# Attention and two feed-forwards: the sign in the weight conversion, and blocks cut by unit

## The chip, the cores and the metric

The kernel runs on one core of one Trainium2 chip. The metric is the device time of one launch in microseconds (us). Before the change three runs gave 1076.47, 1080.43 and 1082.78 us, so the median is 1080.43 us. The core has five engines with their own in-order instruction streams: TensorE (PE: matrix products; PEld is its weight load), VectorE (DVE), ScalarE (ACT), GpSimd (POOL), and SyncE (SP), which here does nothing but issue DMAs.

## The reference

Inputs arrive as 64-bit floating-point numbers. Block-causal attention (4 batches, 8 heads, 576 positions, head size 64, blocks of 64) is followed by two feed-forwards on 2304 tokens with 512 channels and 2048 hidden channels:

```
scores = q @ k.T / sqrt(64);  masked where block(i) < block(j);  attn = softmax(scores);  x = attn @ v
h = x @ moe_w_in;   g = max(0.01 * h, h);                       x = g @ moe_w_out
h = x @ moe2_w_in;  P = a0 + a1 h + a2 h^2 + a3 h^3;  Q = 1 + |b0| |h| + |b1| h^2
out = (P / (Q + 1e-6)) @ moe2_w_out
```

## The kernel before

**Weights.** A weight stays 64 bits wide in memory, and the kernel reads it as two 32-bit words: `hi` (sign, exponent, upper mantissa) and `lo`. It makes a 32-bit float of them and splits this into a rounded part (`w1i`, `w1o`, or `ch` on its way to the memory tensor `w2h`) and a residual `cl` (on its way to `w1l` or `w2l`). The products run on these parts, three per product: high by high, high by low, low by high.

**Conversion.** `convert` works on 64 blocks of 128 x 512 weights: 32 of the first feed-forward, then 32 of the second. One block passes through these steps:
1. a DMA (L148) loads the block into `cs`, of which there are three;
2. the `hi` words, read as floats, are multiplied by 2^-112, in the first 16 blocks by GpSimd (L166), in the other 48 by ScalarE (L168); this moves the exponent and keeps the sign in the top bit;
3. ScalarE scales the `lo` words as integers (L172);
4. VectorE takes the sign bit out of `hi` and puts it into `lo` (L179, the sign operation);
5. VectorE shifts `hi` left by 3 and joins it with `lo` to the float `cl` (L181);
6. ScalarE rounds it (L184), GpSimd subtracts the rounded part (L185);
7. a DMA issue (L156) writes the residual out; of the second feed-forward both parts are written.

`convert` is a generator with two stops per block: steps 2 to 4 are issued ahead of one stop, 5 to 7 behind it (step 4 belongs to the block before). Between the steps of attention `pace` advances it by a table of due steps (`due`). If a unit of the first feed-forward is prepared before its weights are there, `cv_to` advances it further.

**Blocks before.** A block of the input weights is 128 rows by 512 columns: 128 pieces of 4 KB are read. Four such blocks (all 512 rows) serve four units, so a unit waits for a group of four blocks (table `NEED`). A residual is written in 512 pieces of 512 bytes, four to each partition. A block of the second matrix is 128 full rows.

**Attention and the first feed-forward.** 32 heads run one after the other. Per head: scores (`T`, L291 for the first eight heads, L297 after), maxima on VectorE (`nm`, L303), exponentials on ScalarE (`PB`, L309), division by the sums on GpSimd (L319), transposes (L346), copies of the transposed parts (`pTh` on ScalarE, `pTl` on VectorE, L331 to L339), and the product with v (L374, L378), whose result goes to `xh` and `xl` (L391, L392) or first to `vr` (L394, L395). When a batch's eight heads are done, its first feed-forward (`moe1`, products L455) fills TensorE between the steps of the next batch's heads. It has 32 units per batch, "in" (128 hidden channels) and "out" (128 output channels over 512 hidden ones). For each the residual `wl` is loaded by a DMA on SyncE's queue (L429). The products' results pass through ScalarE (L468, a parametric ReLU with slope 0.01, and L469) and VectorE (`gl`, L470; sums `acc`, L475 and L477).

**The second feed-forward** (`moe2`, products L558 and L612) follows when everything above is done, from about 680 us.

**Order.** SyncE's queue is in program order. A scheduler at build time sets the order of the other engines; each then runs strictly in it, so that an instruction that waits holds up all that stand behind it.

Of the kernel before, what the change touches and what calls it, by code (L numbers as in the profile page):

```python
# [8 lines left out]
F32 = mybir.dt.float32  # L9
F32R = mybir.dt.float32r  # L10
# [3 lines left out]
AF = mybir.ActivationFunctionType  # L14
ALU = mybir.AluOpType
# [9 lines left out]
def attention_moe_moe_kernel(  # L25
# [46 lines left out]
    cp = ph1.enter_context(tc.tile_pool(name="cp", bufs=2))  # L72
# [22 lines left out]
    w1i = w1.tile([P, KD, DFF], F32R, name="w1i")  # L95
    w1o = w1.tile([P, NF, DM], F32R, name="w1o")
# [11 lines left out]

    W1L = dram.tile([2 * NF, P, KD, P], F32, name="w1l")
    W2H = dram.tile([NF, P, 2 * KD, P], F32, name="w2h")
    W2L = dram.tile([NF, P, 2 * KD, P], F32, name="w2l")
    NSF = 8
    E1 = "pvpapv"
    blocks = []
    for wi, wo, which in ((w1_in, w1_out, 1), (w2_in, w2_out, 2)):
        for g in (0, 1, 4, 2, 5, 3, 6, 7) if which == 1 else (0, 4, 1, 5, 2, 6, 3, 7):
            for r in range(4):
                if g < 4:  # L120
                    src = wi[r * P:(r + 1) * P, 2 * g * 512:2 * (g + 1) * 512]
                    fs = slice(4 * g, 4 * g + 4)
                    if which == 1:
                        dst = w1i[:, r, g * 512:(g + 1) * 512], W1L[fs, :, r, :]
                    else:
                        dst = W2H[fs, :, r, :], W2L[fs, :, r, :]
                else:
                    f = 4 * (g - 4) + r
                    src = wo[f * P:(f + 1) * P, :]
                    if which == 1:  # L130
                        dst = w1o[:, f, :], W1L[NF + 4 * (g - 4):NF + 4 * (g - 3), :, r, :]
                    else:
                        dst = tuple(W[f:f + 1, :, KD:2 * KD, :] for W in (W2H, W2L))
                blocks.append((src, dst, which == 1))
    stage = {}
    QME = "ap"
    WHOLE = 8
    NPG = range(0, 16)
    NPC = range(0)
    XLE = "p"  # L140
    EP = "a"
    XWA = 0
# [2 lines left out]
    def load_block(i):  # L145
        if i < len(blocks):
            stage[i] = cp.tile([P, 512, 2], I32, tag="cs", name="cs", bufs=3)
            nc.sync.dma_start(out=stage[i].rearrange("p n w -> p (n w)"), in_=blocks[i][0])  # L148

    split = []  # L150

    def write_block():
        if split:
            for d, t in split.pop():
                out = d.rearrange("u p c -> p u c") if len(d.shape) == 3 else d.rearrange("u p d c -> p (u d) c")
                nc.sync.dma_start(out=out, in_=t.rearrange("p (u c) -> p u c", c=P))  # L156
            ndone[0] += 1

    def convert():
        load_block(0)  # L160
        load_block(1)
        for i in range(len(blocks) + 1):
            if i < len(blocks):
                hi, lo = stage[i][:, :, 1], stage[i][:, :, 0]
                if i in NPG:
                    nc.gpsimd.tensor_scalar(hi.bitcast(F32), hi.bitcast(F32), 2.0 ** -112, 1.0, ALU.mult, ALU.mult)  # L166
                else:
                    nc.scalar.activation(hi.bitcast(F32), hi.bitcast(F32), AF.Copy, scale=2.0 ** -112)  # L168
                if i in NPC:
                    nc.gpsimd.tensor_scalar(lo, lo.bitcast(U32), 0.875 * 2.0 ** -29, 0.4375, ALU.mult, ALU.add)  # L170
                else:
                    nc.scalar.activation(lo, lo.bitcast(U32), AF.Copy, scale=0.875 * 2.0 ** -29, bias=0.4375)  # L172
            if i > 0:
                s = stage.pop(i - 1)
                _, (dh, dl), kept = blocks[i - 1]
                hi, lo = s[:, :, 1], s[:, :, 0]
                f = cp.tile([P, 512], F32, tag="cl", name="cl", bufs=3)
                wh = dh if kept else cp.tile([P, 512], F32R, tag="ch", name="ch", bufs=2)
                nc.vector.scalar_tensor_tensor(lo, hi, -(2 ** 31), lo, ALU.bitwise_and, ALU.bitwise_or)  # L179
                yield  # L180
                nc.vector.scalar_tensor_tensor(  # L181
                    f.bitcast(I32), hi, 3, lo, ALU.logical_shift_left, ALU.bitwise_or
                )
                nc.scalar.copy(wh, f)  # L184
                nc.gpsimd.tensor_tensor(f.bitcast(F32R), f, wh.bitcast(F32), ALU.subtract)  # L185
                load_block(i + 1)
                write_block()
                split.append(((dh, wh.bitcast(F32)), (dl, f))[kept:])
                yield
        write_block()  # L190
# [60 lines left out]
    def a1(n):  # L251
# [5 lines left out]
        if n < NSF + 2:  # L257
            split_tiles(n)
        e = n % 2
        qs, ks = qk[e][0:D, :], qk[e][D:P, :]  # L260
        cp1(E1[0], QT[e][0:D, :], qs, SCALE)
        nc.vector.scalar_tensor_tensor(
            QT[e][D:P, :], qs, SCALE, QT[e][0:D, :].bitcast(F32), ALU.mult, ALU.subtract
        )
        cp1(E1[2], QM[e][0:D, :], QT[e][0:D, :].bitcast(F32))
        cp1(E1[3], KH[e][D:P, :], ks)
        cp1(E1[4], KH[e][0:D, :], ks)
        (nc.vector if E1[5] == "v" else nc.gpsimd).tensor_tensor(
            KL[e][0:D, :], ks, KH[e][D:P, :].bitcast(F32), ALU.subtract
# [133 lines left out]
    units = []  # L403
    for b in range(B):
        fs = list(range(NF))
        cuts = [5, 9, 13, 16] if b < B - 1 else [5, 10, 14, 16]
        done = 0
        for g, c in enumerate(cuts):
            units += [(b, "in", f, 0) for f in fs[done:c]]
            done = c  # L410
            units += [(b, "out", g, d) for d in range(KD)]
    NEED = {
        ("in" if g < 4 else "out", g % 4): 4 * (n + 1) for n, g in enumerate((0, 1, 4, 2, 5, 3, 6, 7))
    }
    wt = {}
    prepped = [0]

    def prep_w1(u):
        while prepped[0] <= min(u, len(units) - 1):
            w = prepped[0]  # L420
            ub, kind, i, d = units[w]
            if ub == 0:
                cv_to(NEED["in", i // 4] if kind == "in" else NEED["out", i])
            if kind == "in":
                wh, src = w1i[:, :, i * P:(i + 1) * P], W1L[i]
            else:
                wh, src = w1o[:, 4 * i:4 * i + 4, d * P:(d + 1) * P], W1L[NF + 4 * i + d]
            wl = mp.tile([P, 4, P], F32R, tag="wl", name="wl", bufs=3)
            nc.sync.dma_start(out=wl.bitcast(F32), in_=src)  # L429
            wt[w] = (wh, wl)  # L430
            prepped[0] += 1
# [208 lines left out]
    with tc.manual_schedule(engines={mybir.EngineType.SP}):  # L640
# [50 lines left out]
        for n, (b, h) in enumerate(heads):  # L691
            odd, p = h % 2, n // 2
# [49 lines left out]
        for i in range(16):  # L742
# [3 lines left out]
            if L0 <= i < L0 + NA + 2:  # L746
                f = i - L0
# [49 lines left out]
```

## Time and profile before

| | |
|---|---|
| median of 3 runs | 1080.43 us |
| profiled execution | 1077.4 us, its span 1075.6 us |
| TensorE busy | 1015.4 us (94%) |
| VectorE busy | 770.2 us (72%) |
| ScalarE busy | 661.4 us (61%) |
| GpSimd busy | 314.2 us (29%) |
| mean granted TensorE clock | 0.986 |

The conversions begin at 19.4 us and end near 527 us. Attention with the first feed-forward between its steps ends near 570 us; the rest of the last batch's first feed-forward runs until about 680 us, and the second feed-forward after it. The granted clock is the share of full speed that TensorE was given: 1.0 is 2.4 GHz, 0.5 is 1.2 GHz. "Idle before" counts the time in which an engine had no instruction running, and the engine and line behind the arrow ended it.

### The profile page before, as it was taken

The page shows a single profiled execution, that of the slowest core. Times are in us where ns is not written, and L with a number is a line of the kernel's source. Part 1 is how long each engine was busy: PE and PEld are TensorE (multiplying, and loading weights), DVE is VectorE, ACT ScalarE, POOL GpSimd, SP SyncE. Part 2 cuts the span into 40 slices and gives each one's busy share as a digit, 9 for nine tenths or more (in the row PEclk, how much of TensorE's full clock was granted, in tenths as well). Part 3 has the DMA queues.
Part 4 walks back from the last instruction along what each step waited for, and adds up shares of the span by engine and source line. Part 5 has one row for each costly group of instructions (what it writes and reads, how often), then busy time and mean ns, then how long its engine had stood idle before and what let it go on. Part 6 is the DMA issues. An engine that isn't in the chain of part 4 may idle for free.

```text
span 1075.6 us, 16845 instructions
## 1 busy us (share of the span) xinstructions
PE 1015.4 (94%) x6120; PEld 911.1 (85%) x6120; DVE 770.2 (72%) x1261; ACT 661.4 (61%) x1319; POOL 314.2 (29%) x368
## 2 busy tenths in 40 slices
PE   6878888898999999999999999899999999999998
PEld 4557888898989999999999999788888888888887
DVE  3778778886767775877632222698988888888876
ACT  5766656855756665666632111777776676676675
POOL 5687545555444555545320001100000000000000
PEclk9999899999999999999999999999999999999999
DMA  7458566856766567665445845812000110110010
GB/s 190 135 150 252 155 192 189 261 169 203 218 190 175 185 201 237 200 196 168 145 132 197 329 127 171 340 56 79 4 36 9 70 40 1 40 40 1 1 40 20
DMA packets 99954, 149.01 MB, mean 139 GB/s; under 512 B 8224, under 2 KB 52256, under 8 KB 99872
## 3 DMA queue, kind: packets, MB, share of 16 engines
q1 hardware_dynamic: 99872, 147.95, 43.7%
q8 instruction: 48, 0.79, 0.3%
q14 instruction: 34, 0.28, 0.1%
HBM read 108.01 MB, written 39.32 MB: 137 GB/s over the span
## 4 chain that ended last, share of the span: by engine, by line
PE 53%; issue 11%; DMA 8%; DVE 6%; ACT 3%; POOL 2%; SPq 1%; POOLq 0%; ACTq 0%; DVEq 0%
PE o L612 18%; PE h L558 18%; PE M L455 12%; DMA cs<-in_moe_w_in_dram 4%; DMA cs<-in_moe_w_out_dram 3%; PE T L297 2%; PE T L346 2%; PE T L378 1%; POOL acc L482 1%; DVE cl L181 1%; ACT cs L168 1%; ACT cs L172 1%; DVE cs L179 1%; DVE pTl L339 1%; DVE nm L303 1%
## 5 line engine op out<-in xcount | busy, mean ns | idle before, releaser
L319 POOL TENSOR_SCALAR PB<-PB,sm 128x448 f32<-128x448 f32 (+4 forms) x160 | 104.7, 674 | 58.0 <-DVE sm L316 49.5
L309 ACT ACTIVATE PB<-T,nm 128x448 f32<-128x448 f32 (+4 forms) x160 | 83.1, 524 | 55.8 <-DVE nm L303 52.0
L455 PE MATMUL M<-gh,wl 128*128 128x288 f32 x512 | 114.0, 299 | 1.1 <-DMA wl<-w1l 1.1
L455 PE MATMUL M<-gh,w1o 128*128 128x288 f32 x512 | 113.8, 300 | 1.3 <-DVE pTl L339 0.6
L455 PE MATMUL M<-gl,w1o 128*128 128x288 f32 x512 | 111.6, 298 | 1.0 <-DVE gl L470 1.0
L570 ACT ACTIVATE ea<-h,coef 128x512 f32<-128x512 f32 (+1 forms) x80 | 51.7, 647 | 92.7 <-PE h L558 88.9
L470 DVE TENSOR_TENSOR gl<-M,gh 128x576 fp32r<-128x576 f32 x64 | 47.8, 749 | 65.7 <-ACT M L469 65.6
L558 PE MATMUL h<-x2h,w2h 128*128 128x512 f32 (+1 forms) x240 | 89.6, 373 | 4.1 <-DVE eu L581 3.2
L455 PE MATMUL M<-xh,w1i 128*128 128x288 f32 x512 | 84.6, 299 | 8.5 <-DVE pTl L339 3.8
L179 DVE SCALAR_TENSOR_TENSOR cs<-cs 128x512 int32<-128x512 int32 x64 | 60.1, 938 | 44.7 <-ACT cs L172 33.2
L558 PE MATMUL h<-x2h,w2l 128*128 128x512 f32 (+1 forms) x240 | 89.4, 373 | 0.0
L558 PE MATMUL h<-x2l,w2h 128*128 128x512 f32 (+1 forms) x240 | 89.3, 372 | 0.0
L455 PE MATMUL M<-xl,w1i 128*128 128x288 f32 x512 | 86.0, 301 | 2.2 <-DVE xl L392 1.3
L468 ACT ACTIVATE gh<-M 128x576 fp32r<-128x576 f32 x64 | 41.7, 652 | 75.3 <-PE M L455 75.0
L303 DVE TENSOR_REDUCE nm<-T 128x1 f32<-128x448 f32 (+4 forms) x160 | 71.5, 479 | 21.7 <-PE T L291 13.5
L573 DVE SCALAR_TENSOR_TENSOR ea<-eh,coef,ea 128x512 f32<-128x512 f32 (+1 forms) x80 | 55.9, 699 | 41.4 <-ACT eh L571 40.8
L455 PEld LDWEIGHTS M<-gh,wl 128*128 128x128 f32 x512 | 83.6, 190 | 1.6 <-DMA wl<-w1l 1.6
L455 PEld LDWEIGHTS M<-gh,w1o 128*128 128x128 f32 x512 | 83.0, 190 | 2.2 <-ACT w1i L184 0.8
L612 PE MATMUL o<-w2h,g2l 128*128 128x512 f32 x216 | 84.9, 393 | 0.0
L612 PE MATMUL o<-w2h,g2h 128*128 128x512 f32 x216 | 84.8, 393 | 0.0
L612 PE MATMUL o<-w2l,g2h 128*128 128x512 f32 x216 | 84.6, 392 | 0.0
L455 PEld LDWEIGHTS M<-gl,w1o 128*128 128x128 f32 x512 | 83.1, 190 | 1.3 <-DVE gl L470 1.3
(113 smaller groups left out, 2614.9 us busy)
## 6 DMA issues: line engine op xcount, KB each, us to landing
wl<-w1l SPq DMA_DIRECT2D x128, 256.0 KB, 3.0
cs<-in_moe_w_in_dram SPq DMA_DIRECT2D x32, 512.0 KB, 5.3
cs<-in_moe_w_out_dram SPq DMA_DIRECT2D x32, 512.0 KB, 4.6
w1l<-cl SPq DMA_DIRECT2D x32, 256.0 KB, 5.0
w2h<-ch SPq DMA_DIRECT2D x32, 256.0 KB, 4.9
w2l<-cl SPq DMA_DIRECT2D x32, 256.0 KB, 5.1
w2h<-w2h SPq DMA_DIRECT2D x12, 512.0 KB, 7.4
w2l<-w2l SPq DMA_DIRECT2D x12, 512.0 KB, 8.1
```

The costliest lines, as they stand in the source:

```text
L179: nc.vector.scalar_tensor_tensor(lo, hi, -(2 ** 31), lo, ALU.bitwise_and, ALU.bitwise_or)
L297: nc.tensor.matmul(T[:, po:po + w], lhsT=lhs[e][:, FIRST[i]:FIRST[i] + P], rhs=rhs[e][:, c:c + w], start=(lhs is QT), stop=(lhs is QM),)
L303: nc.vector.tensor_reduce(nm[:, i:i + 1], sc, axis=AX.X, op=ALU.max, negate=True)
L309: nc.scalar.activation(PB[e][i][:, 0:ln], sc, AF.Exp, scale=SCALE if n == 0 else 1.0, bias=nm[:, i:i + 1], accum_out=sm[:, i:i + 1])
L319: nc.gpsimd.tensor_scalar(PB[e][i][:, 0:ln], PB[e][i][:, 0:ln], sm[:, i:i + 1], 1.0, ALU.mult, ALU.mult)
L455: nc.tensor.matmul(T[:, e * 512:e * 512 + NH2], lhsT=w[:, kk, :], rhs=a[:, e * NH2:(e + 1) * NH2], start=(n == 0), stop=(n == 11),)
L468: nc.scalar.activation(gh2, res, AF.Prelu, alpha=0.01)
L470: nc.vector.tensor_tensor(gl2, res, gh2.bitcast(F32), ALU.subtract)
L558: nc.tensor.matmul(h[:, 0:n], lhsT=a, rhs=x, start=(kk == 0 and i == 0), stop=(kk == KD - 1 and i == 2))
L570: nc.scalar.activation(a, h, AF.Abs, scale=coef[:, 4:5])
L573: nc.vector.scalar_tensor_tensor(a, h2, coef[:, 5:6], a, ALU.mult, ALU.add)
L612: nc.tensor.matmul(ob[t], lhsT=a, rhs=w, start=(f == 0 and i == 0), stop=(f == NF - 1 and i == 2))
```

## The change

Three things change in `convert` and what feeds it.

- ScalarE scales the `hi` words of all 64 blocks by a parametric ReLU. The scale is 2^-112 and the slope for negative values -(2^32). A positive word comes out as before. A negative one comes out positive, with its exponent 32 higher; shifted left by 3, that bit of the exponent is the sign bit. The sign operation of VectorE (L179) goes, and the joining operation (L181 before) reads `hi` and `lo` as scaled.
- In the first 16 blocks GpSimd now scales the `lo` words instead of the `hi` words.
- A block is what one unit uses: 512 rows by 128 columns of either matrix of the first feed-forward, listed in the order of the units (32 blocks). Of the second feed-forward a block is 512 rows by 128 columns of the input matrix, or 128 full rows of the output matrix, in turns. Loads of the first three kinds (48 blocks) are in 512 pieces of 1 KB, and every residual and every part of the second feed-forward's weights is written in 128 pieces of 2 KB. A unit of the first batch waits for its own block (`cv_to(w + 1)`).

```
     E1 = "pvpapv"
+    CUTS = [5, 9, 13, 16]
     blocks = []
-    for wi, wo, which in ((w1_in, w1_out, 1), (w2_in, w2_out, 2)):
-        for g in (0, 1, 4, 2, 5, 3, 6, 7) if which == 1 else (0, 4, 1, 5, 2, 6, 3, 7):
-            for r in range(4):
-                if g < 4:
-                    src = wi[r * P:(r + 1) * P, 2 * g * 512:2 * (g + 1) * 512]
...
-                blocks.append((src, dst, which == 1))
+    for g, c in enumerate(CUTS):
+        for f in range(CUTS[g - 1] if g else 0, c):
+            src = w1_in[:, 2 * f * P:2 * (f + 1) * P].rearrange("(r p) w -> p r w", p=P)
+            blocks.append((src, (w1i[:, :, f * P:(f + 1) * P], W1L[f]), True))
+        for d in range(KD):
+            src = w1_out[512 * g:512 * (g + 1), 2 * d * P:2 * (d + 1) * P].rearrange("(r p) w -> p r w", p=P)
+            blocks.append((src, (w1o[:, 4 * g:4 * g + 4, d * P:(d + 1) * P], W1L[NF + 4 * g + d]), True))
+    for f in range(NF):
+        src = w2_in[:, 2 * f * P:2 * (f + 1) * P].rearrange("(r p) w -> p r w", p=P)
+        blocks.append((src, (W2H[f, :, 0:KD, :], W2L[f, :, 0:KD, :]), False))
+        src = w2_out[f * P:(f + 1) * P, :].rearrange("p (r w) -> p r w", r=KD)
+        blocks.append((src, (W2H[f, :, KD:2 * KD, :], W2L[f, :, KD:2 * KD, :]), False))
...
-    NPG = range(0, 16)
-    NPC = range(0)
...
-            nc.sync.dma_start(out=stage[i].rearrange("p n w -> p (n w)"), in_=blocks[i][0])
+            nc.sync.dma_start(out=stage[i].rearrange("p (r n) w -> p r (n w)", r=KD), in_=blocks[i][0])
...
-                out = d.rearrange("u p c -> p u c") if len(d.shape) == 3 else d.rearrange("u p d c -> p (u d) c")
-                nc.sync.dma_start(out=out, in_=t.rearrange("p (u c) -> p u c", c=P))
+                nc.sync.dma_start(out=d, in_=t)
...
-                if i in NPG:
-                    nc.gpsimd.tensor_scalar(hi.bitcast(F32), hi.bitcast(F32), 2.0 ** -112, 1.0, ALU.mult, ALU.mult)
-                else:
-                    nc.scalar.activation(hi.bitcast(F32), hi.bitcast(F32), AF.Copy, scale=2.0 ** -112)
-                if i in NPC:
+                nc.scalar.activation(
+                    hi.bitcast(F32), hi.bitcast(F32), AF.Prelu, scale=2.0 ** -112, alpha=-(2.0 ** 32)
+                )
+                if i < 16:
                     nc.gpsimd.tensor_scalar(lo, lo.bitcast(U32), 0.875 * 2.0 ** -29, 0.4375, ALU.mult, ALU.add)
                 else:
                     nc.scalar.activation(lo, lo.bitcast(U32), AF.Copy, scale=0.875 * 2.0 ** -29, bias=0.4375)
...
-                f = cp.tile([P, 512], F32, tag="cl", name="cl", bufs=3)
-                wh = dh if kept else cp.tile([P, 512], F32R, tag="ch", name="ch", bufs=2)
-                nc.vector.scalar_tensor_tensor(lo, hi, -(2 ** 31), lo, ALU.bitwise_and, ALU.bitwise_or)
+                f = cp.tile([P, KD, P], F32, tag="cl", name="cl", bufs=3)
+                wh = dh if kept else cp.tile([P, KD, P], F32R, tag="ch", name="ch", bufs=2)
+                hi, lo = (x.rearrange("p (r c) -> p r c", c=P) for x in (hi, lo))
                 yield
                 nc.vector.scalar_tensor_tensor(
                     f.bitcast(I32), hi, 3, lo, ALU.logical_shift_left, ALU.bitwise_or
                 )
...
-        cuts = [5, 9, 13, 16] if b < B - 1 else [5, 10, 14, 16]
+        cuts = CUTS if b < B - 1 else [5, 10, 14, 16]
...
-    NEED = {
-        ("in" if g < 4 else "out", g % 4): 4 * (n + 1) for n, g in enumerate((0, 1, 4, 2, 5, 3, 6, 7))
-    }
...
-                cv_to(NEED["in", i // 4] if kind == "in" else NEED["out", i])
+                cv_to(w + 1)
```

Line numbers of the changed kernel are smaller by 4 to 9: the joining operation is L175 there, the maxima L297, `pTl` L333, `gl` L461, `vr` L389, the reciprocal L310.

VectorE before, from 112 to 119 us of the trace (the fourth row is the sixteenth sign operation, whose block is the last that GpSimd scales; `cs` holds the words, `cl` the joined float, `gl` a residual of the first feed-forward, `vr` an attention output):

```order
L316 RECIPROCAL sm<-sm 128x5
L470 TENSOR_TENSOR gl<-M,gh 128x576
L181 SCALAR_TENSOR_TENSOR cl<-cs 128x512
L179 SCALAR_TENSOR_TENSOR cs<-cs 128x512
L181 SCALAR_TENSOR_TENSOR cl<-cs 128x512
L395 TENSOR_TENSOR vr_87<-T,vr_87 64x576
L470 TENSOR_TENSOR gl<-M,gh 128x576
L276 TENSOR_TENSOR VHL_96<-vr_86,VHL_96 128x5x64
```

VectorE in the changed kernel at the same `vr`:

```order
L175 SCALAR_TENSOR_TENSOR cl<-cs 128x512
L310 RECIPROCAL sm<-sm 128x5
L461 TENSOR_TENSOR gl<-M,gh 128x576
L175 SCALAR_TENSOR_TENSOR cl<-cs 128x512
L389 TENSOR_TENSOR vr_87<-T,vr_87 64x576
L461 TENSOR_TENSOR gl<-M,gh 128x576
L270 TENSOR_TENSOR VHL_96<-vr_86,VHL_96 128x5x64
```

Of the four conversion instructions ahead of this `vr` before, both sign operations are gone (the other one stood three rows above this piece); the joining operation of the same block still stands directly ahead of `vr`.

VectorE before, around the transposed parts of a head in the second batch (the 43rd sign operation, at 316.04 us of the trace):

```order
L336 TENSOR_TENSOR pTh<-T,pTh 64x128
L339 TENSOR_TENSOR pTl<-T,pTh 128x768
L339 TENSOR_TENSOR pTl<-T,pTh 128x448
L179 SCALAR_TENSOR_TENSOR cs<-cs 128x512
L339 TENSOR_TENSOR pTl<-T,pTh 128x320
L181 SCALAR_TENSOR_TENSOR cl<-cs 128x512
L470 TENSOR_TENSOR gl<-M,gh 128x576
L303 TENSOR_REDUCE nm<-T 128x1 x2
```

VectorE in the changed kernel at the parts of the same head:

```order
L330 TENSOR_TENSOR pTh<-T,pTh 64x128
L333 TENSOR_TENSOR pTl<-T,pTh 128x768
L175 SCALAR_TENSOR_TENSOR cl<-cs 128x512
L333 TENSOR_TENSOR pTl<-T,pTh 128x448
L461 TENSOR_TENSOR gl<-M,gh 128x576
L333 TENSOR_TENSOR pTl<-T,pTh 128x320
L297 TENSOR_REDUCE nm<-T 128x1 x2
```

The sign operation between the second and third `pTl` is gone. The joining operation of the block before stands between the first and second, and that of this block five rows behind this piece.

## Rows read from the trace of the kernel before

**Rows 1.** The page: busy us (share of span) xinstructions.
```profile
PE 1015.4 (94%) x6120; PEld 911.1 (85%) x6120; DVE 770.2 (72%) x1261; ACT 661.4 (61%) x1319; POOL 314.2 (29%) x368
```

**Rows 2.** Stages: length, busy us by engine, PEclk, DMA share, GB/s.
```profile
10.00:200.00 190.00, 159.01 (x959) 136.01 (x958) 144.59 (x241) 126.26 (x288) 121.04 (x140) 0.95 0.62 188
200.00:570.00 370.00, 353.16 (x2591) 343.60 (x2591) 256.43 (x423) 231.27 (x494) 182.18 (x200) 0.99 0.62 188
```

**Rows 3.** TensorE's waits, 10 to 570 us: total us, times, longest.
```profile
PE T L297 <- DVE vr L395: 9.7, 6, 4.0
...
PE T L346 <- POOL PB L319: 7.1, 10, 4.1
...
PE M L455 <- DMA wl<-w1l: 1.1, 1, 1.1
...
PE T L378 <- DVE acc L329: 0.2, 1, 0.2
```

**Rows 4.** Groups, 0 to 560 us: busy us, mean ns | idle before.
```profile
L179 DVE SCALAR_TENSOR_TENSOR cs<-cs 128x512 int32<-128x512 int32 x64 | 60.1, 938 | 44.7 <-ACT cs L172 33.2 <-POOL cs L166 11.2
...
L181 DVE SCALAR_TENSOR_TENSOR cl<-cs 128x512 int32<-128x512 int32 x64 | 57.7, 903 | 1.1
...
L168 ACT ACTIVATE cs<-cs 128x512 f32<-128x512 f32 x48 | 32.6, 680 | 42.5 <-DMA cs<-in_moe_w_in_dram 24.3 <-DMA cs<-in_moe_w_out_dram 18.1
...
L468 ACT ACTIVATE gh<-M 128x576 fp32r<-128x576 f32 x48 | 31.3, 652 | 5.8 <-PE M L455 5.5
...
L166 POOL TENSOR_SCALAR cs<-cs 128x512 f32<-128x512 f32 x16 | 13.7, 858 | 5.3 <-DMA cs<-in_moe_w_in_dram 5.2
...
L185 POOL TENSOR_TENSOR cl<-cl,w1o 128x512 fp32r<-128x512 f32 x16 | 22.3, 1402 | 20.4 <-ACT w1o L184 18.5 <-issue 1.8
```

**Rows 5.** VectorE's timeline at 115.91: start, us, what [idle].
```profile
115.91 1.74 DVE L179 SCALAR_TENSOR_TENSOR cs<-cs 128x512 int32<-128x512 int32 x1 [2.47 <-POOL cs L166]
```

**Rows 6.** TensorE's timeline, first instruction behind four gaps.
```profile
30.94 0.64 PE L291 MATMUL T<-fk,fq 128*128 128x448 f32 x1 [1.79 <-DVE xl L392]
...
119.09 1.11 PE L297 MATMUL T<-split_fk,split_fq 128*128 128x448 f32 x2 [4.02 <-DVE vr L395]
...
317.28 0.90 PE L455 MATMUL M<-xh,w1i 128*128 128x288 f32 x5 [1.97 <-DVE pTl L339]
...
503.50 0.52 PE L297 MATMUL T<-split_fk,split_fq 128*128 128x192 f32 x3 [1.86 <-DVE pTl L339]
```

**Rows 7.** VectorE's timeline, 316 to 317 us.
```profile
316.04 0.69 DVE L179 SCALAR_TENSOR_TENSOR cs<-cs 128x512 int32<-128x512 int32 x1 [3.27 <-ACT cs L172]
316.65 0.48 DVE L339 TENSOR_TENSOR pTl<-T,pTh 128x320 fp32r<-128x320 f32 x1
```

**Rows 8.** ScalarE's waits, 0 to 570 us: total us, times, longest.
```profile
ACT cs L168 <- DMA cs<-in_moe_w_in_dram: 24.3, 13, 4.0
ACT cs L168 <- DMA cs<-in_moe_w_out_dram: 18.1, 11, 3.5
```

**Rows 9.** Stages, first and last of five at half clock.
```profile
76.77:83.60 6.83, 5.42 (x13) 3.30 (x13) 6.75 (x13) 3.16 (x11) 3.56 (x6) 0.50 0.22 31
...
264.50:267.92 3.42, 3.42 (x17) 3.42 (x16) 0.84 (x2) 1.44 (x3) 2.21 (x2) 0.50 0.82 269
```

**Rows 10.** DMA issues: count, KB each, median us to landing.
```profile
wl<-w1l SPq DMA_DIRECT2D x128, 256.0 KB, 3.0
...
cs<-in_moe_w_in_dram SPq DMA_DIRECT2D x32, 512.0 KB, 5.3
...
w1l<-cl SPq DMA_DIRECT2D x32, 256.0 KB, 5.0
...
x2hd<-xo SPq DMA_DIRECT2D x16, 288.0 KB, 2.5
...
vr<-in_v_dram SPq DMA_DIRECT2D x16, 256.0 KB, 3.0
...
x2l<-x2ld SPq DMA_DIRECT2D x4, 1024.0 KB, 7.7
```

More of the change, by code (lines that the diff above doesn't have):

```diff
@@ L115, in attention_moe_moe_kernel @@
     E1 = "pvpapv"
+    CUTS = [5, 9, 13, 16]
     blocks = []
-    for wi, wo, which in ((w1_in, w1_out, 1), (w2_in, w2_out, 2)):
-        for g in (0, 1, 4, 2, 5, 3, 6, 7) if which == 1 else (0, 4, 1, 5, 2, 6, 3, 7):
-            for r in range(4):
-                if g < 4:
-                    src = wi[r * P:(r + 1) * P, 2 * g * 512:2 * (g + 1) * 512]
-                    fs = slice(4 * g, 4 * g + 4)
-                    if which == 1:
-                        dst = w1i[:, r, g * 512:(g + 1) * 512], W1L[fs, :, r, :]
-                    else:
[L126 to L133, printed above, removed]
-                blocks.append((src, dst, which == 1))
+    for g, c in enumerate(CUTS):
[10 more added lines that the diff above has]
+        blocks.append((src, (W2H[f, :, KD:2 * KD, :], W2L[f, :, KD:2 * KD, :]), False))
     stage = {}
@@ L164, in convert @@
                 hi, lo = stage[i][:, :, 1], stage[i][:, :, 0]
-                if i in NPG:
-                    nc.gpsimd.tensor_scalar(hi.bitcast(F32), hi.bitcast(F32), 2.0 ** -112, 1.0, ALU.mult, ALU.mult)
-                else:
-                    nc.scalar.activation(hi.bitcast(F32), hi.bitcast(F32), AF.Copy, scale=2.0 ** -112)
-                if i in NPC:
+                nc.scalar.activation(
+                    hi.bitcast(F32), hi.bitcast(F32), AF.Prelu, scale=2.0 ** -112, alpha=-(2.0 ** 32)
+                )
+                if i < 16:
                     nc.gpsimd.tensor_scalar(lo, lo.bitcast(U32), 0.875 * 2.0 ** -29, 0.4375, ALU.mult, ALU.add)
```

## The prediction, made before the change was run

> **What bounds the kernel now.** I read the page first, then a table by stage, then who ends TensorE's waits, then the rows around those waits.
>
> TensorE is busy for 1015.4 of 1075.6 us [rows 1], so a change can only give back its idle time and the time it runs at the lower of its two clock levels. The table by stage shows where both lie: busy 159.0 of 190 us from 10 to 200 us and 353.2 of 370 from there to 570 us, that is 31.0 + 16.8 = 47.8 us idle, and granted clocks of 0.95 and 0.99 there [rows 2]. All 64 weight conversions run in this stretch; behind it nothing is converted and this change has nothing to move.
>
> Who ends these waits: fourteen rows name VectorE, from 9.7 us down to 0.2 us, together 29.3 us; the other engines end less (GpSimd 7.1 us at most in a row), and a DMA of the second operand `wl` 1.1 us [rows 3]. VectorE is not full. It is late because it works strictly in order and a conversion stands in its way: the sign operation (L179) runs 64 times for 60.1 us and VectorE sits idle for 44.7 us ahead of it, until ScalarE or GpSimd has scaled the words. The operation behind it (L181, 57.7 us) has 1.1 us of idle time [rows 4].
>
> Two places show how that reaches TensorE. At 115.91 L179 has kept VectorE idle for 2.47 us, until GpSimd's L166; it runs 1.74 us, L181 and `vr` (L395) are queued behind it [rows 5], and TensorE has idled 4.02 us for that `vr` [rows 6]. At 316.04 L179 starts after 3.27 us of idle time, until ScalarE's L172, and the 0.48 us of `pTl` behind it [rows 7] end 1.97 us of TensorE [rows 6].
>
> I went back from every TensorE gap of over 0.5 us between 10 and 570 us by the same steps. There are 26, 40.3 us together. In 21 of them, from the one that ends at 30.94 to the one that ends at 503.50 [rows 6], L179 lies on the chain; they hold 32.7 us. The other five (a coefficient load at the start, two queues of GpSimd, a ScalarE wait, a `wl` load) the change does not touch.
>
> **The change part by part.** The profiled execution took 1077.4 us (span 1075.6); the runs have a median of 1080.43, so it lies 3.0 us under that and inside their spread. The sum is made against 1077.4.
>
> *The sign operation goes.* 64 instructions, 60.1 us of VectorE, and the place at which VectorE waits. In each of the 21 gaps I take the smaller of the gap and L179's own runs on its chain: 25.7 us. If the wait ahead of it goes too, all 32.7 us go. The changed order gives the wait back at the later of the two places (nothing of the conversion stands between the second and third `pTl` any more), but not at the earlier one: there the joining operation still stands ahead of `vr` and still waits for GpSimd.
>
> What is late next differs. In nine gaps (16.0 us whole, 15.5 by the runs) the chain goes back through VectorE and GpSimd; with the one at 119.09 cut to its 1.74 us, since GpSimd's word stays in its place, I take 13.7 us. In twelve (16.7 whole, 10.3 by the runs) it goes back through ScalarE's in-order wait for a weight load ahead of L168, 24.3 + 18.1 = 42.4 us in 24 waits [rows 8], which the change keeps; there `pTh`, `PB` or `gh` on ScalarE is late next, and I take half of the runs, 5.2 us. Sum 18.9.
>
> *The clock.* Five stretches at half clock (1.2 GHz), 23.9 us long together, start around the ends of the five gaps at 76.34, 119.09, 141.53, 199.21 and 263.85, all with a conversion on their chain; TensorE is busy 21.1 us in them, first and last shown [rows 9]. At 2.4 GHz that work takes half, so at most 10.6 us come back. Shorter gaps, not none, are forecast, so I take half: 5.3.
>
> *Float scaling goes from GpSimd (16 blocks) and ScalarE's Copy (48) to a parametric ReLU on ScalarE; the integer scaling of 16 blocks goes to GpSimd.* ScalarE trades 16 instructions against 16. A parametric ReLU is in the trace: 652 ns for 128x576 against 680 ns of L168 for 128x512 [rows 4], so 64 of them cost between 1.8 us less and nothing more: 0 taken. GpSimd's integer form isn't shown. Nearest is L166, 858 ns, dearest L185 with its two inputs, 1402; so between 0 and 16 x 0.54 = 8.7 us more; a gain is left out, since L166 has the same shape and the same pair of operations. I take 0, by L166; the cover is GpSimd's slack (121.0 busy of 190 us, [rows 2]), and without it up to 8.7 us come on the path, between 20 and 115 us.
>
> *The fused operation waits later.* It now waits for ScalarE and GpSimd itself; queued behind it are `vr`, `xl`, `pTl` and the maxima `nm`, which TensorE and the exponentials wait for. That is the same queue that L179 held up, half a conversion step later, by when ScalarE is mostly past it: 0, and the upper end is the gap between 25.7 and 32.7 already left out.
>
> *Blocks of one unit.* Units need one block instead of four at once; TensorE has hardly waited for it (1.1 us for `wl`, at the end of the stage, [rows 3]): 0. The loads come in pieces of 1 KB instead of 4 KB (48 of 64), the residuals go out in pieces of 2 KB instead of 512 bytes. For loads the rows bound it: 256 KB take 3.0 us in pieces of 512 bytes (`vr`) and 3.0 in pieces of 2 KB (`wl`): nothing, and no row shows more pieces as faster; at the dear end the slowest load with as many pieces, `x2l`, takes 7.7 us against 5.3 of the weights: +2.4 [rows 10]. Twelve gaps of 16.7 us hang on those 42.4 us, 0.39 us of TensorE for each. I take +0.4 us, near the first pair, in the 24 waits there are: 24 x 0.4 x 0.39 = 3.8 us lost. Writes are off TensorE's path: 0, though `w1l` at 5.0 us against 2.5 for `x2hd` [rows 10] leaves something to gain.
>
> The Trainium skill ("DMA: Bandwidth & Descriptors", Specifications) puts the least size for full rate at 512 bytes; by it neither the loads nor the writes would change, and the sum would be 3.8 us better. The pair `vr`, `wl` agrees for loads. The pair `w1l`, `x2hd` does not for writes.
>
> Sum: 18.9 + 5.3 - 3.8 = 20.4 us. 1077.4 - 20.4 = 1057.0, and at the level of the median 1080.4 - 20.4 = 1060.0; the profile lies under its median by less than the runs scatter, so I name 1059.
>
> **The rivals.**
> - *The waits only move* (no change). The fused operation takes over L179's 44.7 us of waiting, and what VectorE saves is idle time. For it: the words it waits for are made no sooner. Against it: it stands later in VectorE's order. Only the gaps without a wait ahead of L179 (four, ending at 80.03, 94.16, 172.25 and 182.91) would go, 3.9 us, and no clock: 1076.5.
> - *The loads in 1 KB pieces* (slower). Each load lands later and ScalarE, in order, waits at the head of every block, with the exponentials and `pTh` behind it. At the dear end, 24 x 2.4 x 0.39 = 22.5 us lost; the twelve gaps then give nothing and the clock half of its share: 22.5 - 13.7 - 2.6 = 6.2 us slower, 1087. It decides from loads 16.3/(24 x 0.39) = 1.7 us later on; under that the kernel is faster. Against it: the pair of rows with equal landing times.
> - *GpSimd's integer form is dear.* 8.7 us on the path, at the half of the span where it is fullest: 1068.
> - *All of it comes back*: 32.7 + 10.6 = 43.3 us, 1037. Against it: the ScalarE waits for loads stay.
> - *The ReLU does not come cheap* (a table load each time): excluded nearly, since the same function already runs among the exponentials with 5.5 of its 5.8 us of idle time owed to TensorE [rows 4].
>
> **How the numbers follow.** The forecast 0.55, all of it 0.12, GpSimd dear 0.11, waits only move 0.13, loads slow 0.09. What runs can tell from no change is about 0.5%, 5.4 us. Faster: 0.55 + 0.12 + 0.11 = 0.78. Same: 0.13. Slower: 0.09. The range goes from 1041, most of the way to the best case, to 1079, which takes in the unchanged case but not the slow one. The forecast's own range is 1049 to 1068.
>
> **What would show it.** Right: VectorE's instructions fall by 64 and its busy time by 55 to 65 us; idle time ahead of the fused operation under 25 us; TensorE's idle time from 10 to 570 us near 28 us; fewer stretches at half clock before 300 us. GpSimd's integer scaling under 1 us, the ReLU near 0.68, weight loads landing within 0.5 us of 5.3. Wrong: idle time of 40 us before the fused operation (the waits moved), ScalarE waiting over 60 us for weight loads (the pieces), or GpSimd's scaling at over 1.3 us.

## The result, and the profile after

The change makes the kernel faster by about 12 us: four runs have a median of 1066.05 us (1062.72 to 1071.16), before it was 1080.57; the ratio of the two kernels is put at 0.9885 with a 95% interval of 0.985 to 0.9919, that is 8.8 to 16.2 us (the medians alone lie 14.5 us apart). The forecast was 1059 with a range of 1041 to 1079: the direction and the range held, the gain by the ratio was 60% of the 20.4 us worked out.

The changed kernel's page, busy time by engine, beside [rows 1]:

```profile
PE 1012.0 (95%) x6120; PEld 908.7 (85%) x6120; DVE 714.5 (67%) x1197; ACT 658.7 (62%) x1319; POOL 300.8 (28%) x368
```

VectorE has 64 instructions and 55.7 us less, as counted on. The span fell from 1075.6 to 1064.6 us: TensorE's busy time by 3.4 us, its idle time by 7.6.

The stages, with the columns of [rows 2], and the first and the last of the three stretches at half clock that are left of the five (both kernels have one more near 16 us, ahead of the conversions):

```profile
10.00:200.00 190.00, 170.72 (x1059) 147.82 (x1057) 126.59 (x228) 137.13 (x312) 123.38 (x147) 0.96 0.66 206
200.00:565.00 365.00, 345.24 (x2548) 336.63 (x2547) 221.11 (x375) 220.72 (x475) 166.43 (x193) 1.00 0.59 183
78.10:84.90 6.80, 6.25 (x24) 4.88 (x23) 4.28 (x11) 4.61 (x12) 4.76 (x7) 0.50 1.01 351
...
252.20:255.60 3.40, 3.40 (x17) 3.40 (x16) 0.04 (x1) 1.25 (x3) 1.05 (x1) 0.50 0.94 349
```

Up to 200 us TensorE idles 190 - 170.7 = 19.3 us, 11.7 less than before. Behind that it idles 365 - 345.2 = 19.8 us, 3.0 more. So the gain lies in the first 200 us, and a part of it is given back later.

The conversion's own rows, with the columns of [rows 4]:

```profile
L175 DVE SCALAR_TENSOR_TENSOR cl<-cs 128x512 int32<-128x512 int32 x64 | 51.1, 799 | 72.2 <-DMA w2l<-cl 26.8 <-ACT cs L166 25.5 <-POOL cs L164 14.7
...
L160 ACT ACTIVATE cs<-cs 128x512 f32<-128x512 f32 x64 | 43.4, 678 | 58.3 <-DMA cs<-in_moe_w_out_dram 31.2 <-DMA cs<-in_moe_w_in_dram 26.9
...
L164 POOL TENSOR_SCALAR cs<-cs 128x512 int32<-128x512 uint32 x16 | 12.6, 787 | 3.6 <-DMA cs<-in_moe_w_in_dram 2.0 <-DMA cs<-in_moe_w_out_dram 0.5
```

The parametric ReLU costs 678 ns, what Copy cost, and GpSimd's integer form 787 ns, under the 858 of its float form. But VectorE's idle time ahead of the joining operation is 72.2 us, where the sign operation had 44.7: the waits did not go, they moved to the operation that is left, and 26.8 us of waiting for a free residual buffer came to them. ScalarE's waits for weight loads rose from 42.4 to 58.1 us. TensorE's idle time from 10 us to the end of the conversions is 39 us; the prediction had named 28, before it was 47.8.

What ScalarE's wait for a load does now, at 339 us: ScalarE, VectorE and TensorE in order of time (start, us, what, idle before):

```profile
336.42 0.67 ACT L160 ACTIVATE cs<-cs 128x512 f32<-128x512 f32 x1 [3.31 <-DMA cs<-in_moe_w_out_dram]
336.99 0.89 ACT L325 CAST pTh<-T 128x896 fp32r<-128x896 f32 x1
```
```profile
337.91 0.28 DVE L330 TENSOR_TENSOR pTh<-T,pTh 64x128 fp32r<-64x128 f32 x1 [4.35 <-ACT pTh L325]
338.21 0.96 DVE L333 TENSOR_TENSOR pTl<-T,pTh 128x768 fp32r<-128x768 f32 x1
```
```profile
339.31 0.64 PE L291 MATMUL T<-split_fk,split_fq 128*128 128x192 f32 x4 [1.59 <-DVE pTl L333]
```

ScalarE stands 3.31 us at the head of a block, `pTh` is queued behind it, `pTl` needs `pTh`, and TensorE loses 1.59 us. VectorE had nothing to do for 4.35 us. Before, at 316 us, such a wait reached TensorE through the sign operation [rows 7].

The DMA issues, beside [rows 10]:

```profile
cs<-in_moe_w_in_dram SPq DMA_DIRECT2D x32, 512.0 KB, 4.9
cs<-in_moe_w_out_dram SPq DMA_DIRECT2D x32, 512.0 KB, 5.7
w1l<-cl SPq DMA_DIRECT2D x32, 256.0 KB, 4.9
```

### The profile page after: what moved, and what is told of

Same layout as the page of the kernel before. It is cut to its first block, busy times and chain, and to the rows that moved or that the text cites. A ratio compares the mean times of both kernels' runs of the same rounds, so it can differ in the third digit from the quotient of the medians.

```text
span 1064.6 us, 16750 instructions
## 1 busy us (share of the span) xinstructions
PE 1012.0 (95%) x6120; PEld 908.7 (85%) x6120; DVE 714.5 (67%) x1197; ACT 658.7 (62%) x1319; POOL 300.8 (28%) x368
## 4 chain that ended last, share of the span: by engine, by line
PE 47%; issue 15%; DMA 13%; ACT 8%; DVE 7%; POOL 6%; SPq 4%; POOLq 0%; DVEq 0%; ACTq 0%
PE o L603 19%; PE h L549 18%; PE M L446 7%; DMA cs<-in_moe_w_out_dram 5%; DMA w2l<-cl 3%; DMA cs<-in_moe_w_in_dram 2%; POOL PB L313 2%; ACT PB L303 2%; PE T L340 1%; DMA x2hd<-xo 1%; ACT cs L160 1%; SPq L235 1%; PE T L372 1%; ACT cs L166 1%; POOL cl L179 1%
## 5 line engine op out<-in xcount | busy, mean ns | idle before, releaser
L313 POOL TENSOR_SCALAR PB<-PB,sm 128x448 f32<-128x448 f32 (+4 forms) x160 | 92.2, 596 | 60.4 <-DVE sm L310 49.7
L175 DVE SCALAR_TENSOR_TENSOR cl<-cs 128x512 int32<-128x512 int32 x64 | 51.1, 799 | 72.2 <-DMA w2l<-cl 26.8
L461 DVE TENSOR_TENSOR gl<-M,gh 128x576 fp32r<-128x576 f32 x64 | 48.1, 754 | 72.3 <-ACT M L460 70.9
L564 DVE SCALAR_TENSOR_TENSOR ea<-eh,coef,ea 128x512 f32<-128x512 f32 (+1 forms) x80 | 55.7, 696 | 43.2 <-ACT eh L562 42.6
L446 PE MATMUL M<-xh,wl 128*128 128x288 f32 x512 | 82.4, 298 | 2.3 <-DMA wl<-w1l 2.3
L340 PE MATMUL T<-ident,PB 128*128 128x128 f32 x480 | 70.5, 285 | 14.5 <-POOL PB L313 7.1
```

Source lines behind the costliest of these rows:

```text
L175: nc.vector.scalar_tensor_tensor(f.bitcast(I32), hi, 3, lo, ALU.logical_shift_left, ALU.bitwise_or)
L313: nc.gpsimd.tensor_scalar(PB[e][i][:, 0:ln], PB[e][i][:, 0:ln], sm[:, i:i + 1], 1.0, ALU.mult, ALU.mult)
L340: nc.tensor.transpose(T[:, c:c + P], PB[e][i][:, kt * P:(kt + 1) * P], ident)
L446: nc.tensor.matmul(T[:, e * 512:e * 512 + NH2], lhsT=w[:, kk, :], rhs=a[:, e * NH2:(e + 1) * NH2], start=(n == 0), stop=(n == 11),)
L461: nc.vector.tensor_tensor(gl2, res, gh2.bitcast(F32), ALU.subtract)
L564: nc.vector.scalar_tensor_tensor(a, h2, coef[:, 5:6], a, ALU.mult, ALU.add)
```

## The experiments

Every kernel ran in rounds beside the kernel before; ratios are to that kernel, 1080 us.

| run | what it is | ratio (95%) |
|---|---|---|
| | the change | 0.9885 (0.985 to 0.9919) |
| e1 | sign alone moved | 0.9827 (0.9797 to 0.9857) |
| e2 | blocks alone | 1.0035 (1.0017 to 1.0053) |
| e3 | sign operation kept, issued late | 0.9978 (0.9962 to 0.9994) |
| e4 | the change, loads one block earlier | 0.9784 (0.9755 to 0.9812) |
| e5 | e1 with an extra operation of two inputs | 0.9949 (0.993 to 0.9967) |
| e6 | e1 with an extra maximum of `hi` | 0.9884 (0.9851 to 0.9918) |
| e7 | e1, loads one block earlier | 0.9812 (0.9786 to 0.9838) |
| e8 | e7, residuals written earlier | 0.9849 (0.9829 to 0.9869) |
| e9 | before, loads one block earlier | 0.9978 (0.9961 to 0.9995) |
| e10 | e2, loads one block earlier | 0.9979 (0.9955 to 1.0003) |
| e11 | the change, GpSimd scales nothing | 0.9821 (0.9794 to 0.9848) |
| e12 | e1 with an extra maximum of `cl` | 0.9895 (0.9872 to 0.9918) |

**The two halves, e1 and e2.** Theory 1: the sign operation is the gain. Theory 2: the blocks are. e1 is the kernel before with

```
-                if i in NPG:
...
-                    nc.scalar.activation(hi.bitcast(F32), hi.bitcast(F32), AF.Copy, scale=2.0 ** -112)
-                if i in NPC:
+                nc.scalar.activation(
+                    hi.bitcast(F32), hi.bitcast(F32), AF.Prelu, scale=2.0 ** -112, alpha=-(2.0 ** 32)
+                )
+                if i < 16:
...
-                nc.vector.scalar_tensor_tensor(lo, hi, -(2 ** 31), lo, ALU.bitwise_and, ALU.bitwise_or)
```

> Blocks, loads and waits by groups of four stay as before; only the sign moves into the parametric ReLU (and GpSimd scales the integer words of the first 16 blocks). Theory 1, the freed sign operation is the whole gain: 1064 to 1070 us, ratio to before 0.985 to 0.991, VectorE's busy time 55 us lower. Theory 2, the blocks of one unit make the gain: 1077 to 1082 us, ratio 0.997 to 1.003.

e2 is the changed kernel with the scaling and the sign operation of before put back.

> The sign operation and the scaling stay as before; only the blocks are cut by unit (loads in 1 KB pieces, writes in 2 KB pieces, a unit waits for its own block). Theory 1: 1078 to 1084 us, ratio 0.997 to 1.004, with ScalarE's waits for weight loads near 55 us as in the changed kernel if the pieces cost something. Theory 2: 1064 to 1070 us, ratio 0.985 to 0.991.

Measured: 1063.52 and 1084.44 us. Theory 1 holds: the sign is worth 18.7 us (15.4 to 21.9), and the blocks cost 3.8 (1.8 to 5.7). The product of the two ratios is 0.9861, and the change's 0.9885 has it in its interval. Both times lie just outside what theory 1 had named (1064 to 1070 and 1078 to 1084 us): the sign gains more than the whole change, and the blocks cost. The stages of e1, then of e2, then the second stage of before cut at the same time:

```profile
10.00:200.00 190.00, 168.03 (x1031) 145.48 (x1029) 124.78 (x224) 135.14 (x306) 123.73 (x148) 0.96 0.67 203
200.00:562.00 362.00, 346.67 (x2575) 338.36 (x2575) 221.71 (x378) 224.69 (x480) 165.89 (x192) 1.00 0.61 188
```
```profile
10.00:200.00 190.00, 159.18 (x958) 135.87 (x957) 143.17 (x239) 122.72 (x283) 117.02 (x139) 0.95 0.60 185
200.00:562.00 362.00, 341.35 (x2480) 332.45 (x2481) 260.36 (x421) 229.67 (x493) 174.66 (x198) 0.98 0.58 184
```
```profile
200.00:562.00 362.00, 345.71 (x2535) 336.15 (x2534) 255.64 (x422) 228.88 (x490) 179.32 (x198) 0.99 0.62 187
```

The blocks cost nothing up to 200 us (30.8 us idle, 31.0 before); behind it TensorE idles 20.7 us with them and 16.3 before, and the granted clock is 0.98. In e1 it idles 9.0 us less than before up to 200 us and 1.0 us less behind. ScalarE's groups with the waits for weight loads, e1 first, then e2:

```profile
L165 ACT ACTIVATE cs<-cs 128x512 f32<-128x512 f32 x64 | 43.5, 680 | 59.1 <-DMA cs<-in_moe_w_in_dram 29.6 <-DMA cs<-in_moe_w_out_dram 29.3
```
```profile
L163 ACT ACTIVATE cs<-cs 128x512 f32<-128x512 f32 x48 | 32.6, 678 | 38.9 <-DMA cs<-in_moe_w_out_dram 21.1 <-DMA cs<-in_moe_w_in_dram 17.5
```

So these waits rose with the sign's move and not with the pieces: 58.9 us in e1, whose loads are in 4 KB pieces, and 38.6 in e2, with 48 of 64 loads in 1 KB pieces, against 42.4 before. The expectation of near 55 us in e2 failed, and the blocks' 3.8 us do not come by longer waits of ScalarE for loads. e2 changes the pieces of the loads, the pieces of the writes and what a unit waits for at once; which of them costs was not run by itself.

**Wait or running time: e3, e5, e6, e12.** The prediction held that the sign operation hurt by standing at the head of VectorE's queue. Theory A: its wait is the price. Theory B: its 60 us of running are. e3 moves the operation behind the stop:

```
-                nc.vector.scalar_tensor_tensor(lo, hi, -(2 ** 31), lo, ALU.bitwise_and, ALU.bitwise_or)
                 yield
+                nc.vector.scalar_tensor_tensor(lo, hi, -(2 ** 31), lo, ALU.bitwise_and, ALU.bitwise_or)
```

> The kernel before with the sign operation kept (60 us of VectorE) and only issued behind the stop, right ahead of the joining operation. If the place of the wait held TensorE up: idle time ahead of the sign operation falls from 44.7 us, and the time comes down to 1064 to 1072 us. If the 60 us of running did: 1075 to 1082 us.

Measured: 1077.83 us, but the edit did not do what it was for. The wait ahead of the sign operation stayed, 41.2 us against 44.7 (the group of e3, with the columns of [rows 4]):

```profile
L180 DVE SCALAR_TENSOR_TENSOR cs<-cs 128x512 int32<-128x512 int32 x64 | 58.7, 917 | 41.2 <-ACT cs L172 31.6 <-POOL cs L166 9.0
```

So it tells nothing of the wait. e5 goes the other way: it leaves the sign to the ReLU and adds an operation that waits for nothing, and e6 and e12 one with a single input (each run has one of the three added lines):

```
                 nc.vector.scalar_tensor_tensor(
                     f.bitcast(I32), hi, 3, lo, ALU.logical_shift_left, ALU.bitwise_or
                 )
+                nc.vector.scalar_tensor_tensor(lo, hi, 0, lo, ALU.bitwise_and, ALU.bitwise_or)    # e5
+                nc.vector.tensor_reduce(junk, hi.bitcast(F32), axis=AX.X, op=ALU.max)             # e6
+                nc.vector.tensor_reduce(junk, f, axis=AX.X, op=ALU.max)                           # e12
```

> The kernel with the sign alone moved (1063.5 us), plus one VectorE operation per block right behind the joining one: lo = (hi and 0) or lo, the same shape and two inputs as the old sign operation, with nothing left to wait for. If the 60 us of running were the price of the sign operation: back to 1074 to 1082 us. If its wait at the head of the queue was: 1062 to 1068 us.

> As the run with the extra operation, but the extra one is a maximum over the hi words: one input, about the same VectorE time. If VectorE's own queue is what the running costs: 1074 to 1082 us as there. If the price is that an operation with two inputs holds GpSimd up: GpSimd's divisions keep their 600 ns (670 ns in the run with two inputs) and the time stays at 1062 to 1068 us.

> The sign alone moved (1063.5 us) plus a maximum over the joined words directly behind the joining operation: one input, nothing to wait for, 64 runs of 0.6 to 0.7 us. If VectorE's time itself is the price: near the 1073 us of the extra operation with two inputs, at least 1070. If what two inputs do to GpSimd is: 1062 to 1067 us, GpSimd's divisions near 613 ns.

Measured: e5 1073.41, e6 1067.39, e12 1068.65 us. First e1's groups of the joining operation and of GpSimd's divisions, then those of e5, e6 and e12 with the extra operation:

```profile
L317 POOL TENSOR_SCALAR PB<-PB,sm 128x448 f32<-128x448 f32 (+4 forms) x160 | 95.0, 613 | 52.8 <-DVE sm L314 43.9 <-ACT gh L466 8.4 <-PE T L289 0.2
...
L179 DVE SCALAR_TENSOR_TENSOR cl<-cs 128x512 int32<-128x512 int32 x64 | 51.4, 804 | 58.9 <-DMA w2l<-cl 23.0 <-ACT cs L171 16.4 <-POOL cs L169 11.8
```
```profile
L318 POOL TENSOR_SCALAR PB<-PB,sm 128x448 f32<-128x448 f32 (+4 forms) x160 | 105.6, 679 | 57.9 <-DVE sm L315 49.0 <-ACT gh L467 8.6
...
L182 DVE SCALAR_TENSOR_TENSOR cs<-cs 128x512 int32<-128x512 int32 x64 | 63.9, 999 | 0.8
...
L179 DVE SCALAR_TENSOR_TENSOR cl<-cs 128x512 int32<-128x512 int32 x64 | 53.4, 834 | 46.4 <-DMA w2l<-cl 20.2 <-ACT cs L171 10.3 <-POOL cs L169 7.9
```
```profile
L180 DVE SCALAR_TENSOR_TENSOR cl<-cs 128x512 int32<-128x512 int32 x64 | 53.0, 828 | 16.3 <-POOL cs L170 7.4 <-ACT cs L172 4.4 <-DMA w1l<-cl 3.4
...
L183 DVE TENSOR_REDUCE junk<-cs 128x1 f32<-128x512 f32 x64 | 43.5, 680 | 47.3 <-ACT cs L166 47.0
```
```profile
L319 POOL TENSOR_SCALAR PB<-PB,sm 128x448 f32<-128x448 f32 (+4 forms) x160 | 96.6, 622 | 55.9 <-DVE sm L316 44.5 <-ACT gh L468 8.4 <-PE T L291 2.7
...
L180 DVE SCALAR_TENSOR_TENSOR cl<-cs 128x512 int32<-128x512 int32 x64 | 53.5, 836 | 54.0 <-DMA w2l<-cl 27.0 <-ACT cs L172 8.6 <-POOL cs L170 8.3
...
L183 DVE TENSOR_REDUCE junk<-cl 128x1 f32<-128x512 f32 x64 | 43.5, 679 | 0.8
```

e5's time lies 0.6 us under the range for the running time and 5.4 over the one for the wait. In it an operation with 0.8 us of idle time ahead of it takes back 0.9949 - 0.9827 = 0.0122 of the time, 13.2 of the 18.7 us. VectorE's idle time ahead of a conversion's operations did not rise with it: 58.9 us in e1, 46.4 + 0.8 = 47.2 in e5, 44.7 + 1.1 = 45.8 before [rows 4]. The time goes up as this idle time goes down; what goes up with the time is the running. That is theory B, for 13.2 of the 18.7 us.

e6 turned into a test of the wait's place, because its maximum, which needs `hi` alone, runs ahead of the joining operation. So 47.3 us are waited at the first operation and 16.3 at the second, where e12 waits 54.0 and 0.8. Both run the same 43.5 us more than e1 and cost nearly the same, 6.2 and 7.3 us. A price of the place at which VectorE waits is not to be seen in the time, but the two times are only known to some 4 us against each other: e6's six executions fall into two groups, 1060 to 1064 and near 1071 us, and its trace is of the fastest. None of these runs takes the waits away, so what they would be worth altogether stays open.

Of the 13.2 us, e12 with its single input has 7.3, between its two ranges, so neither VectorE's time nor the hold on GpSimd comes out as the whole price. A part of the 7.3 can be another dependency: in e12 GpSimd waits 10.7 us until the maximum has read its words; e6 has no such wait and costs 6.2. The other 5.8 us come with the second input and with what it brings, 20.4 us more of running (63.9 against 43.5). GpSimd shows a reason: its 160 divisions take 613 ns in e1, 622 in e12 and 679 in e5. In the kernel before, which also has 64 operations of two inputs more, they take 674:

```profile
L319 POOL TENSOR_SCALAR PB<-PB,sm 128x448 f32<-128x448 f32 (+4 forms) x160 | 104.7, 674 | 58.0 <-DVE sm L316 49.5 <-ACT gh L468 8.4
```

While an operation with two inputs runs beside GpSimd, each seems to hold the other up (the extra one takes 999 ns in e5, the maximum 679). All runs fit this: the divisions take 642 to 697 ns in the six kernels that have the sign operation or e5's in its stead, and 581 to 622 in the eight others. The last 5.5 us of the 18.7 these runs do not assign; the wait at the head of the queue, theory A, may have its part there.

**Earlier loads: e4, e7, e9, e10.** Is it ScalarE's in-order wait for loads that holds the gain down? One edit on four kernels:

```
         load_block(1)
+        load_block(2)
...
-                load_block(i + 1)
+                load_block(i + 2)
```

> The changed kernel with each weight load issued one block earlier (the same three buffers; the load then waits on its queue for the joining operation of the block before last). If ScalarE's in-order waits for loads (58 us in the changed kernel) are what holds the gain down: they fall under 15 us and the time goes to 1050 to 1060 us. If something else is late next, or the queue's own wait delays the other loads: 1063 to 1070 us.

> The sign alone moved, blocks of before, and each weight load issued one block earlier. If the blocks of one unit cost some 4 us and the earlier load is worth 9 us by itself, both independent: 1050 to 1057 us, under the 1056.7 of the changed kernel with the earlier load. If the earlier load only repairs what the blocks cost: 1060 to 1066 us.

> The kernel before with each weight load issued one block earlier, nothing else. If the earlier load is worth something by itself wherever ScalarE waits for loads (42 us here): 1068 to 1075 us. If, as beside the moved sign (ratio 0.9812 against 0.9827), it is worth next to nothing with the old blocks: 1077 to 1082 us.

> The blocks cut by unit with the old sign operation, and each load issued one block earlier. If the blocks cost their 4 us by late loads, the earlier load takes that back: 1070 to 1079 us, ratio under 0.999. If they cost it in another way: 1081 to 1086 us.

Measured: 1056.71, 1060.95, 1077.27 and 1077.85 us. With the old blocks the earlier load is worth 2.4 us (e9 against before) and 1.6 (e7 against e1, not clear of noise). With the blocks of one unit it is worth 6.0 (e10 against e2) and 10.9 (e4 against the change). With it the blocks cost nothing: 0.9979 against 0.9978 with the old sign, 0.9784 against 0.9812 with the new. So what the blocks cost hangs on when the loads are issued, and e7, e9 and e10 came out as the theory has it by which the earlier load only repairs what the blocks cost. e4's time is in the range for ScalarE's waits, but the way of it is not the one expected. The groups of e4:

```profile
L176 DVE SCALAR_TENSOR_TENSOR cl<-cs 128x512 int32<-128x512 int32 x64 | 55.7, 871 | 56.6 <-DMA w2l<-cl 38.3 <-DMA w1l<-cl 12.4 <-POOL cs L165 5.2
...
L161 ACT ACTIVATE cs<-cs 128x512 f32<-128x512 f32 x64 | 43.6, 682 | 59.0 <-DMA cs<-in_moe_w_in_dram 36.5 <-DMA cs<-in_moe_w_out_dram 22.3
```

ScalarE still waits 59.0 us for loads, not under 15. Gone are VectorE's waits for ScalarE's words (25.5 us) and most of those for GpSimd's (14.7 to 5.2); its waits for a free residual buffer rose from 28.3 to 50.7 us instead. Which of these the blocks' cost came through stays open.

**Free the residual buffer sooner: e8.** With the same three buffers the write is issued earlier:

```
+                write_block()
                 yield
...
-                write_block()
```

> As the run before, and the residual of a block is written out half a conversion step earlier. If VectorE's waits for a free residual buffer (the writes of w1l and w2l; 51 us in the changed kernel with the earlier load) reach TensorE: they fall below 30 us and the time is 3 to 8 us lower than without. If they are covered: the same within 2 us.

Measured: 1063.91 us, 4 us slower than e7. The waits for the buffer went from 34.9 to 24.8 us, as wanted, and the time went up, as neither theory had it. So they do not reach TensorE in a way that shows in the time, and the earlier write costs something else. ScalarE's waits for a free buffer of the rounded part rose from 6.4 us in e7 to 15.5; whether that is the cost was not tested.

**GpSimd's share: e11.**

```
-                if i < 16:
+                if i < 0:
```

> The changed kernel with ScalarE scaling the integer words of the first 16 blocks too, so GpSimd loses 16 operations (12.6 us) and ScalarE gains 16 of 0.67 us. If GpSimd's share holds TensorE up between 20 and 115 us: 1058 to 1064 us. If ScalarE is the tighter one there: 1068 to 1076 us.

Measured: 1060.91 us, ratio 0.9821 against 0.9885: ScalarE doing all the scaling is 6.9 us faster than the change (2.2 to 11.6, taking the two intervals together). The 14.7 us that VectorE waited for GpSimd's words are gone, although ScalarE has 16 operations more; all of VectorE's idle time ahead of the joining operation went from 72.2 to 66.2 us only. What such a wait does shows at 108 us of the change, on GpSimd, VectorE and TensorE:

```profile
105.52 2.57 POOL L313 TENSOR_SCALAR PB<-PB,sm 128x448 f32<-128x448 f32 x5
108.18 0.66 POOL L164 TENSOR_SCALAR cs<-cs 128x512 int32<-128x512 uint32 x1
```
```profile
108.87 0.69 DVE L175 SCALAR_TENSOR_TENSOR cl<-cs 128x512 int32<-128x512 int32 x1 [3.25 <-POOL cs L164]
```
```profile
111.71 0.92 PE L291 MATMUL T<-split_fk,split_fq 128*128 128x448 f32 x3 [2.41 <-DVE vr L389]
```

In e11 the gap ahead of that `vr` is 0.79 us, and of the stretches at half clock that the change has at 78 and 112 us neither is there. Its first stage:

```profile
10.00:200.00 190.00, 170.26 (x1092) 148.38 (x1091) 128.77 (x237) 149.36 (x337) 113.81 (x135) 0.99 0.68 209
```

TensorE idles 19.7 us in it, as much as in the change (19.3), but at a granted clock of 0.99 instead of 0.96 it gets 1092 products done instead of 1059. So in the two profiled executions the gain up to 200 us is one of the clock.

Whether the 6.9 us are the price of GpSimd's share stays open: e1 has the same share, with the blocks of before, and is as fast as e11 (0.9827 against 0.9821). The loss that the blocks add and the one that e11 takes away may be the same one; e1 with the edit of e11 was not run.

The fastest of all is e4, 1056.71 us, faster than both kernels. e4 with the edit of e11 was not run.

## Why the prediction was right, and where it was not

**Right: TensorE pays for the sign operation.** The 21 gaps were found by going back along the chain, and the sum took L179's running time in them as its measure, not the wait ahead of it. e5 supports that choice: the running alone takes back 13.2 of 18.7 us. For the other 5.5 no run decides between the wait and the running.

**Wrong: the account of VectorE's wait.** The prediction said that VectorE is late because a conversion waits at the head of its queue, and wanted under 25 us ahead of the joining operation. It measured 72.2 us, more than before, which the text gave as the sign of its rival "the waits only move" at 1076.5. They did move, and the time fell all the same. That rival failed with the same premise, that VectorE's idle time is what TensorE pays for. The runs give it the other sign: 45.8 us ahead of a conversion's operations before, 58.9 in e1, which is 1.7% faster. Nor did the later of the two places come free, where nothing of the conversion was to stand between the second and third `pTl`. The joining operation of the block before now waits between the first and the second, for a free residual buffer, and TensorE idles 0.67 us behind it, where it was 1.97:

```profile
302.70 0.83 DVE L175 SCALAR_TENSOR_TENSOR cl<-cs 128x512 int32<-128x512 int32 x1 [2.67 <-DMA w2l<-cl]
```

**Too large: the gaps and the clock.** 18.9 + 5.3 = 24.2 us were named for the sign; e1 gives 18.7. TensorE's busy time fell from 1015.4 to 1011.8 us in e1 (1012.0 in the change), so the clock gave back 3.6 us instead of 5.3; the stretches at half clock went from 23.9 to 13.6 us in the change. The gaps gave the rest: about 15 us of the 18.7 by the runs, and 10.3 us of idle time in the profiled executions of before and e1, whose spans lie only 13.9 us apart; 18.9 were named. The two parts of it went differently. Up to 200 us e1 got 9.0 us of idle time back and the change 11.7, not far from the 13.7 of the nine gaps that went through VectorE and GpSimd. Behind 200 us, where most of the twelve gaps behind a ScalarE load wait lie, half of the runs was forecast (5.2); e1 got 1.0 us back, and the change, with the blocks, lost 3.0. There `pTh` and `PB` took the sign operation's place, as named, and took nearly all of that gain: in e1 TensorE's waits behind 200 us that `pTl` ended went from 6.6 to 5.6 us only, and those that `PB` ended rose from 0.7 to 2.9. The half of these twelve gaps is the term that was sized too high by most.

**Right in size by luck: the blocks.** 3.8 us of loss were set down for loads in 1 KB pieces, by 0.4 us later landing and 24 waits. e2 measured 3.8 us, but its ScalarE waits for loads are shorter than before (38.6 against 42.4 us), and loads do not land 0.4 us later throughout: in the change the input weights 4.9 us against 5.3, the output weights 5.7 against 4.6 (half of these are still in 4 KB pieces), and in e4 with the same pieces 5.3 and 4.7. The loss goes when the loads are issued earlier (e10, e4), with the same pieces; by which way it comes stays open. The rival of slow loads, decided from 1.7 us on, is out.

**Wrong: the writes.** From `w1l` at 5.0 us and `x2hd` at 2.5 [rows 10] I read that pieces of 512 bytes are slow to write. In pieces of 2 KB `w1l` lands after 4.9 us. So the pair of rows was misread: the two DMAs differ in more than their pieces. The Trainium skill ("DMA: Bandwidth & Descriptors", Specifications) puts the least size for full rate at 512 bytes; these rows agree.

**Missed: GpSimd's place.** The trade between GpSimd and ScalarE was put at 0, with GpSimd's integer form as its only risk. The form is cheap, 787 ns. But the word waits behind five divisions for its turn (at 105.52 us above), as L166 had done at 115 us [rows 5]. The prediction kept that wait as given and saw no choice in it; e11, which takes the wait and 12.6 us of GpSimd's time away together, is 6.9 us faster. That the queue and not the running is what costs was not tested by itself.

## What to carry to other kernels

When an operation on the chain has a wait ahead of it, price its running time and its hold on other engines first, and test the wait by itself before counting it: adding an operation that waits for nothing is a short edit, and shows what the running time alone costs. An operation given to an engine because that engine has slack still stands in its queue, so look at what is queued ahead of it. And measure the two halves of a change apart: here one half cost a third of what the change gained, and issuing the loads one block earlier took it back.

## What the runs showed of the hardware that was not expected

- VectorE's operation with two inputs from the on-chip memory and GpSimd's divisions seem to slow each other: 674 and 679 ns per division with 64 more of them (before, e5), 613 and 622 without (e1, e12). The operation takes 651 to 1774 ns in e5. The maximum with one input over the same 512 columns takes 647 to 689 ns in e12, and the divisions beside it 622.
- The Trainium skill ("SBUF — State Buffer", SBUF: two separate sides) says that a VectorE operation with two inputs from that memory and a GpSimd one that reads it take a shared pair of ports in turns, each for its whole length. The runs agree that both get longer (not how they take turns), and e5 costs 5.8 us more than e12 for 64 operations.
- Loads of 512 KB in 512 pieces of 1 KB land no later than in 128 pieces of 4 KB: the input weights after 4.5 to 5.3 us (e2, the change, e10, e4) against 5.3 and 5.5 (before, e1). Writes of 256 KB gain nothing clear from 2 KB instead of 512 bytes: `w1l` lands after 4.7 to 5.1 us in the same four runs, against 5.0 and 5.1.
